# A long convolution by Fourier stages with a gated convolution behind it: late outputs, the order of products and taps, and the source of the taps

## The chip, the cores and the metric

The kernel runs on one core of one Trainium2 chip. The core has TensorE (PE, with PEld for its weight loads), VectorE (DVE), ScalarE (ACT), GpSimd (POOL) and SyncE (SP), which here issues every DMA. The metric is device microseconds per execution; the median of several runs counts.

## The reference

Eight sequences x[b] of 6400 x 128 are convolved with one long filter h of 6400 x 128, channel by channel (an FFT of double length, cut to 6400). What comes out, a, goes through a gated layer:

```
y    = irfft(rfft(x, 2S) * rfft(h, 2S))[:S]              # per channel
pre  = sum over k<5 of conv_w[k] * y[t-4+k]              # a short causal convolution, per channel
out  = (sigmoid(pre) * (y @ w_val)) @ w_out
```

All is float32.

## The kernel before

The long convolution is done as a real transform of length 6400 = 100 x 64, in four matrix stages on PE. The spectrum of h is computed once. For each of the eight sequences (batches) there are two stages in the program, and PE, DVE, ACT and POOL all keep the written order of their own instructions.

**First stage**, 16 groups (`for g in range(NS)`, line 584). Each group does the third transform of this batch (`s3_quads`: 64 matmuls from `gy` into two single PSUM banks, copied to `dt` by ACT and by DVE) and the first transform of the next batch (`fx.half`, 16 times 2 matmuls from `sd` into a pair of banks, copied to `gy` by ACT). POOL makes the sums and differences `sd` of the loaded x for it (`fx.sums`).

**Second stage**, 13 steps (`for s in range(NCH)`, line 611). Each step has

- a *product* for the next batch: the second transform on PE (`Product`, into a PSUM pair, of which there are two), two multiplications with the filter's spectrum on DVE (`mul_u` writes `gy`, `mul_t` writes `h`), and two additions on POOL (`add`, `gy` from `gy` and `h`);
- a *chunk* of this batch's result: the fourth transform on PE (`s4`, from `m4_sb` and `dt` into a single bank). The chunks are the head (positions 60 to 63 of 64) and 1 to 12, of five positions each.

What follows a chunk is the gated layer. ACT makes `copies` (y, to SBUF, in `dt` or `yl`, and two of the five taps of the short convolution, times their weights, one of them into the small buffer `p`). DVE adds three more *taps* (`more`: SCALAR_TENSOR_TENSOR, out = in x weight + out), POOL adds the fifth from `p`. PE projects y by w_val (`project`), ACT applies the sigmoid (`sigm`), DVE multiplies (`gate`), PE multiplies by w_out (`output`), ACT copies the result and SP stores it (`store`). A chunk's taps run one step after its fourth transform, its projection and gate two after, its output three after, its store four after.

Chunks 8 to 12 (positions 35 and up) are *late* in all batches but the last: in the second stage they are only copied to `yl`, and taps, projection, gate, output and store of these five and of the head come in the next batch's first stage (`Gates.trail`).

PSUM has four single banks, handed out in turn to the third transform, fourth transform, projection and output; a bank is free when its last reader is done. The taps of chunks that are not late, and of the head, read their chunk's PSUM bank.

Before the first batch there is a prologue: the first transform of h and of batch 0, and then, step by step, the spectrum of h and the products of batch 0. Between these products DVE decodes the gated layer's weights from their eight-byte form (`weights`, two operations a step). The tables of the fourth transform (`m4_sb`, thirteen pieces of 375 KB) are loaded in the first stage of batch 0, one a group.

Of the kernel before, what the change touches and what calls it, by code (L numbers as in the profile page):

```python
# [16 lines left out]
C = 128  # L17
# [3 lines left out]
HR = N1 // 2  # L21
HP = 64
MW = 3 * HR
SB = 4
NKB = 13
TAPS = 5
# [3 lines left out]
CH = 5  # L30
HEAD = (60, 4)
CHUNKS = [HEAD] + [(a, CH) for a in range(0, 60, CH)]
NCH = len(CHUNKS)
# [3 lines left out]
M2B = 3  # L37
# [73 lines left out]
def longconv_moe(ctx: ExitStack, tc: tile.TileContext, x, h, r1, m2, r3, m4, w64, out):  # L111
# [185 lines left out]
    class Spectrum:  # L297
# [72 lines left out]
    class Chunk:  # L370
# [33 lines left out]
        def copies(self):  # L404
            a, n = self.ch
            if a == HEAD[0]:
                for i, o in cells(0, n):
                    nc.gpsimd.memset(o[:, :, :1], 0.0)
                    self.first(4, o[:, :, 1:], self.p[:, i : i + n, : N1 - 1])
                act(self.y, self.p)  # L410
                for i, o in cells(a, n):
                    self.first(0, o, self.p)
                return
            if self.late:
                act(self.y, self.p)
                self.p = self.y
                return
            self.init()
            act(self.y, self.p)
            self.q = p_t[a // CH % 2]  # L420
            self.first(3, self.q, self.p)

        def init(self):
            a, n = self.ch
# [51 lines left out]
                        self.o[k * HP : (k + 1) * HP, i : i + o.shape[1]], lhsT=w, rhs=o, start=True, stop=True  # L476
                    )

        def store(self):
            act(self.y, self.o)  # L480
            i, k = _out_range(self.ch)
            nc.sync.dma_start(out[self.b, i:k].rearrange("(e n t) -> e n t", e=C, n=self.ch[1]), self.y)

# [25 lines left out]
    for kb in range(MH):  # L509
        m2_load(kb, m2_head)  # L510
    nc.sync.dma_start(r3_sb, r3)
    sp, pr = {0: Spectrum(0)}, {}
    for kb in range(-1, NKB + 1):
        if 0 <= kb < NKB:
            pr[kb] = Product(kb, sp[kb].h, t_head[kb % 3], m2_head)
            m2_load(kb + MH, m2_head)
        if kb + 2 < NKB:
            sp[kb + 2] = Spectrum(kb + 2)
        if kb + 1 < NKB:
            sp[kb + 1].copy()  # L520
            sp[kb + 1].store()
        if 0 <= kb < NKB:
            pr[kb].mul_u()
            pr[kb].mul_t()
            pr[kb].add(nc.vector if kb == NKB - 1 else nc.gpsimd)
            next(wgen, None)
            next(wgen, None)
    pairs.pop([p is ps2 for p in pairs].index(False))
    psp.__exit__(None, None, None)
    ps1 = ctx.enter_context(tc.tile_pool(name="ps1", bufs=4, space=bass.MemoryType.PSUM))  # L530

    class Gates:


        def __init__(self, b, defer):
            self.cs = [Chunk(b, ch, defer) for ch in CHUNKS]

        def trail(self):

            h, late = self.cs[0], [c for c in self.cs if c.late]  # L540
            steps = collections.defaultdict(list)
            for m, c in enumerate(late + [h]):
                t = 2 * m + 2
                if c is not h:
                    steps[t - 2].append(lambda c=c: c.taps(range(2)))
                    steps[t - 1].append(lambda c=c: c.taps(range(2, 4)))
                steps[t] += [c.project, c.sigm, c.gate]
                steps[t + 2].append(c.output)
                steps[t + 3].append(c.store)
            n = max(steps)  # L550
            return [lambda c=steps[i]: [f() for f in c] for i in range(n + 1)]

        def at(self, s, last):

            return self.cs[s] if 1 <= s < NCH else self.cs[0] if s == NCH and last else None

        def each(self, what, s, last=True):
            c = self.at(s, last)
            if c and not c.late:
                getattr(c, what)()  # L560

        def finish(self, s):
            self.each("project", s - 2)
            self.each("output", s - 3)
            self.each("store", s - 4)
            self.each("sigm", s - 2)
            if s == NCH:
                self.cs[NCH - 1].taps()
            self.each("gate", s - 2)

    trail = []
    fx = Forward(x[1], gy) if B > 1 else None
    if fx:
        fx.load(XB)
    for b in range(B):
        nxt = b + 1 < B


        if trail:
            trail.pop(0)()  # L580
        if nxt:
            for _ in range(2):
                fx.sums(nc.gpsimd)
        for g in range(NS):
            e = s3_quads(4 * g)
            f = []
            if nxt:
                f = fx.half()
                fx.sums(nc.gpsimd)
            e[0](act)  # L590
            e[1](dve)
            for u in f:
                u(act)
            if b == 0 and g < NKB:
                a = CH * g
                nc.sync.dma_start(m4_sb[:, a : a + CH], m4.rearrange("k (n t) -> k n t", t=MW)[:, a : a + CH])
            if nxt and g % 2 and g > 1:
                kb = g // 2 - 1
                if kb < M2B:
                    m2_load(kb)  # L600
                else:
                    h_load(kb - M2B)
            if trail:
                trail.pop(0)()
        if b + 2 < B:
            fx = Forward(x[b + 2], gy)


        gs = Gates(b, nxt)
        ps = {}  # L610
        for s in range(NCH):
            if s == 0:
                gs.cs[0].s4()
                gs.cs[0].copies()
                if nxt:
                    ps[0] = Product(0)
                    m2_load(M2B)
            if s == 1:
                gs.cs[s].s4()
            if nxt and s + 1 < NKB:  # L620
                ps[s + 1] = Product(s + 1)
                m2_load(s + 1 + M2B)
            gs.each("project", s - 2)
            if s > 1:
                gs.cs[s].s4()
            gs.each("output", s - 3)
            gs.each("store", s - 4)
            gs.each("sigm", s - 2)
            if s:
                gs.cs[s].copies()  # L630
            if nxt:
                ps[s].mul_u()
            if s > 1 and not gs.cs[s - 1].late:
                gs.cs[s - 1].taps()
            if nxt:
                ps[s].mul_t()
                ps.pop(s).add()
                h_load(s + HB)
            if s == 0:
                gs.cs[0].taps()  # L640
            gs.each("gate", s - 2)
            if s == 10 and b + 2 < B:
                fx.load(XB)
        trail = gs.trail() if nxt else [lambda s=s: gs.finish(s) for s in range(NCH, NCH + 5)]
    for t in trail:
        t()


def _lay_x(v):
# [42 lines left out]
```

## Time and profile before

| what | us |
|---|---|
| median of three runs | 1004.82 (1004.13 to 1008.4) |
| profiled execution, its own time | 1006.82 |
| its span | 1005.0 |
| first stage of the first batch (97.1 to 154.0) | 56.9 |
| usual first stage (328.5 to 380.9) | 52.4 |
| usual second stage (267.5 to 328.5) | 61.0 |
| last first stage, last second stage (900.8 to 946.4 to 1001.6) | 45.6, 55.2 |

A row of the page or of a view of groups gives engine, operation, what it writes and reads, sizes and count, then busy time, the mean ns of one, and the idle time of the engine before these instructions with what ended it. A row of a timeline gives start, duration, engine, operation, names, sizes and count, with an idle time before it in brackets. All instructions are issued through one helper, so that the line is the same for all (L98, and L99 in the changed kernel); names of tiles tell them apart.

### The profile page before, as it was taken

The numbers are of one execution on the slowest core, as the hardware profiler recorded it, in microseconds if no ns is written. First come the engines' busy times: TensorE is split into PE (matmuls) and PEld (weight loads), VectorE is DVE, ScalarE is ACT, GpSimd is POOL, SyncE is SP. The second block draws the span as 40 slices with busy tenths as digits, with TensorE's granted clock in tenths as the row PEclk, the third lists the DMA queues.
The fourth block names the chain that finished last, engine by engine and source line by source line (L and its number), as shares of the span: only waits on it lengthen the run. The fifth ranks groups of instructions, "written<-read, shape, count | busy, mean of one in ns | idle before, by whom it ended". The sixth has DMA issues, their size and how long they took to land.

```text
span 1005.0 us, 46982 instructions
## 1 busy us (share of the span) xinstructions
PE 940.5 (94%) x21360; PEld 793.5 (79%) x21360; DVE 702.8 (70%) x939; ACT 475.5 (47%) x916; POOL 544.5 (54%) x551
## 2 busy tenths in 40 slices
PE   7897778999999999999999998999989999999987
PEld 7797778787978878887878778887887878786753
DVE  5499217977398747977398756977399755978366
ACT  4521434445543653546444554445544553534465
POOL 6467434785277744785177743784367752760032
PEclk9898999999999999999999999999999999999989
DMA  7783854756467545755467555665467554750012
GB/s 253 244 272 149 283 204 158 225 157 194 134 229 214 156 154 194 230 159 166 150 223 218 153 159 186 216 176 170 145 211 221 151 178 159 229 140 34 31 42 91
DMA packets 96838, 177.33 MB, mean 176 GB/s; under 512 B 43392, under 2 KB 49792, under 8 KB 96640
## 3 DMA queue, kind: packets, MB, share of 16 engines
q1 hardware_dynamic: 96640, 174.34, 55.6%
q8 instruction: 167, 2.74, 1.1%
q14 instruction: 31, 0.25, 0.1%
HBM read 141.55 MB, written 32.77 MB: 173 GB/s over the span
## 4 chain that ended last, share of the span: by engine, by line
PE 90%; issue 5%; DVE 3%; POOL 1%; ACT 1%; DMA 0%; POOLq 0%; DVEq 0%; ACTq 0%
PE pt L98 90%; DVE gl L98 1%; DVE dt L98 1%; POOL gl L98 1%; ACT dt L98 1%; DVE gy L98 0%; POOL dt L98 0%; DMA x<-hl 0%; DVE sd L98 0%; DVE m_sb L98 0%; POOLq L688 0%; ACT gl L98 0%; ACT yl L98 0%; ACT gy L98 0%; DVEq L98 0%
## 5 line engine op out<-in xcount | busy, mean ns | idle before, releaser
L98 PE MATMUL pt<-r_sb,gy 64*64 64x128 f32 (+1 forms) x8192 | 267.3, 273 | 20.3 <-issue 11.5
L98 PEld LDWEIGHTS pt<-r_sb,gy 64*64 64x64 f32 (+1 forms) x8192 | 235.8, 130 | 63.8 <-ACT gl L98 20.4
L98 POOL TENSOR_TENSOR sd<-x 128x256 f32<-128x256 f32 x236 | 197.4, 860 | 154.2 <-issue 124.2
L98 POOL TENSOR_TENSOR gy<-gy,h 128x512 f32<-128x512 f32 (+1 forms) x182 | 221.6, 1241 | 63.6 <-DVE h L98 27.7
L98 ACT COPY dt<-pt 128x512 f32<-128x512 f32 (+3 forms) x269 | 155.2, 581 | 193.9 <-PE pt L98 191.6
L98 PEld LDWEIGHTS pt<-m_sb,dt 128*64 128x64 f32 x4096 | 191.5, 137 | 35.3 <-issue 22.7
L98 PEld LDWEIGHTS pt<-gy,m 128*64 128x64 f32 x3008 | 179.1, 135 | 43.8 <-issue 23.6
L98 PE MATMUL pt<-gy,m 128*64 128x128 f32 x3008 | 193.3, 278 | 17.5 <-issue 12.0
L98 PE MATMUL pt<-m_sb,dt 128*64 128x100 f32 x4096 | 198.0, 250 | 2.9 <-DVE dt L98 2.4
L98 DVE COPY dt<-pt 128x512 f32<-128x512 f32 (+1 forms) x136 | 92.5, 680 | 132.1 <-PE pt L98 125.6
L98 PE MATMUL pt<-r_sb,sd 50*64 50x100 f32 x4608 | 143.2, 258 | 17.2 <-issue 11.2
L98 DVE TENSOR_TENSOR gy<-pt,h 128x1024 f32<-128x1024 f32 (+1 forms) x99 | 116.8, 1180 | 46.3 <-PE pt L98 46.3
L98 DVE SCALAR_TENSOR_TENSOR gl<-yl,w_sb,gl 128x500 f32<-128x500 f32 x147 | 130.6, 892 | 24.6 <-ACT gl L98 22.1
L98 PEld LDWEIGHTS pt<-r_sb,sd 50*64 50x64 f32 x4608 | 128.9, 142 | 22.2 <-issue 14.5
L98 DVE SCALAR_TENSOR_TENSOR dt<-pt,w_sb,dt 128x500 f32<-128x500 f32 (+7 forms) x216 | 132.9, 631 | 13.5 <-POOL dt L98 3.8
L98 ACT COPY gy<-pt 128x400 f32<-128x400 f32 x248 | 110.2, 496 | 41.2 <-PE pt L98 32.8
L98 ACT ACTIVATE dt<-pt,w_sb 128x500 f32<-128x500 f32 (+1 forms) x64 | 40.0, 625 | 170.2 <-PE pt L98 169.4
L98 PE MATMUL pt<-dt,w_sb 128*64 128x500 f32 (+2 forms) x480 | 116.0, 561 | 0.8 <-DVE dt L98 0.4
L98 POOL TENSOR_TENSOR dt<-dt,p 128x500 f32<-128x500 f32 (+1 forms) x64 | 66.4, 1038 | 82.5 <-DVE dt L98 58.0
L98 DVE TENSOR_TENSOR h<-pt,h 128x1024 f32<-128x1024 f32 (+1 forms) x91 | 107.3, 1179 | 2.3
L98 ACT COPY yl<-pt 128x500 f32<-128x500 f32 (+1 forms) x96 | 54.5, 568 | 83.9 <-PE pt L98 83.9
L98 DVE TENSOR_TENSOR gl<-pt,gl 128x500 f32<-128x500 f32 (+1 forms) x48 | 31.7, 661 | 54.5 <-PE pt L98 50.8
(40 smaller groups left out, 568.5 us busy)
## 6 DMA issues: line engine op xcount, KB each, us to landing
m<-m SPq DMA_DIRECT2D x90, 512.0 KB, 4.7
h<-hd SPq DMA_DIRECT2D x84, 512.0 KB, 3.9
x<-xl SPq DMA_DIRECT2D x118, 256.0 KB, 3.4
out<-dt SPq DMA_DIRECT2D x56, 250.0 KB, 5.8
out<-yl SPq DMA_DIRECT2D x40, 250.0 KB, 2.5
m_sb<-m SPq DMA_DIRECT2D x13, 375.0 KB, 4.5
hd<-h SPq DMA_DIRECT2D x8, 512.0 KB, 5.1
m_sb<-m SPq DMA_DIRECT2D x6, 512.0 KB, 6.5
```

The lines of the kernel that those rows point to most:

```text
L98: return self._tc.keep_in_program_order(call(*args, **kwargs))
```

## The change

It has these parts.

1. Of the six outputs that stood in the next batch's first stage, those of late chunks 11 and 12 and of the head now stand in that batch's second stage, at its steps 0 and 1. The head's projection and gate come at group 13 of the first stage. The head's result is stored from one of the `p` buffers.
2. In a step of the second stage the two multiplications and POOL's additions now come ahead of the taps of the chunk before; the head's taps come at step 1, behind the second product, and not at step 0.
3. `copies` sets the chunk's source to the SBUF copy y, so that DVE's taps read it and not PSUM.
4. The weights' decode moves from the prologue's products to the first stage of batch 0. Four of the table loads move ahead, into the prologue's products, four stay in that first stage and five move to the second stage of batch 0.
5. In the last batch, DVE's copies of the third transform go to ACT, and projections start at step 5 of the second stage, by a list of steps.

```diff
@@ class Chunk: copies
-                return
-            if self.late:
+            else:
                 act(self.y, self.p)
-                self.p = self.y
-                return
-            self.init()
-            act(self.y, self.p)
-            self.q = p_t[a // CH % 2]
-            self.first(3, self.q, self.p)
+                if not self.late:
+                    self.init()
+                    self.q = p_t[a // CH % 2]
+                    self.first(3, self.q, self.p)
+            self.p = self.y
@@ prologue's products
+    def m4_load(j):
+        a = slice(CH * j, CH * j + CH)
+        nc.sync.dma_start(m4_sb[:, a], m4.rearrange("k (n t) -> k n t", t=MW)[:, a])
+
+    m4_rest = [12, 11, 10, 9, 4, 8, 5, 7, 6]
...
             pr[kb].add(nc.vector if kb == NKB - 1 else nc.gpsimd)
-            next(wgen, None)
-            next(wgen, None)
+        if 0 <= kb < M4H:
+            m4_load(kb)
@@ the first stage
+        for m, c in enumerate(pend[1:]):
+            steps[2 * m] += [lambda c=c: c.taps(range(2))]
+            steps[2 * m + 1] += [lambda c=c: c.taps(range(2, 4))]
+            steps[2 * m + 2] += [c.project, c.sigm, c.gate]
+            if m < 3:
+                steps[2 * m + 4] += [c.output]
+                steps[2 * m + 5] += [c.store]
+        if pend:
+            steps[13] += [pend[0].project, pend[0].sigm, pend[0].gate]
...
-            e[1](dve)
+            e[1](dve if nxt else act)
...
-            if b == 0 and g < NKB:
-                a = CH * g
-                nc.sync.dma_start(m4_sb[:, a : a + CH], m4.rearrange("k (n t) -> k n t", t=MW)[:, a : a + CH])
+            if b == 0:
+                next(wgen, None)
+                next(wgen, None)
+                if g % 3 == 0 and g < 12:
+                    m4_load(m4_rest.pop(0))
@@ the second stage
+        for i, c in enumerate(cs):
+            if i and not c.late:
+                jobs[i + 2 if nxt else (5, 6, 7, 8, 9, 10, 11, 11, 12, 13, 13, 14)[i - 1]].append(c)
+        if not nxt:
+            jobs[NCH + 1].append(cs[0])
...
+            if s == 0 and pend:
+                pend[0].output()
+                pend[0].store(p_t[1][:, : HEAD[1]])
...
+            late = pend[4 + s : 5 + s] if s < 2 else []
+            for c in outs + late:
+                c.output()
...
-            if nxt:
+            if s in ps:
                 ps[s].mul_u()
-            if s > 1 and not gs.cs[s - 1].late:
-                gs.cs[s - 1].taps()
-            if nxt:
                 ps[s].mul_t()
                 ps.pop(s).add()
                 h_load(s + HB)
-            if s == 0:
-                gs.cs[0].taps()
-            gs.each("gate", s - 2)
+            if 0 < s <= NCH and not cs[s - 1].late:
+                cs[s - 1].taps()
+            for c in jobs[s]:
+                c.gate()
```

How it moves instructions is seen at three places. On DVE, steps 4 and 5 of a second stage, before (`pt` is PSUM, `h` and `gy` belong to the product, `dt` holds y and the gate):

```order
TENSOR_TENSOR gy<-pt_2463,h_82 128x2x64x8
SCALAR_TENSOR_TENSOR dt<-pt_2484,w_sb,dt 128x5x100 x3
TENSOR_TENSOR h_82<-pt_2463,h_82 128x1024
TENSOR_TENSOR dt<-pt_2539,dt 128x5x100
TENSOR_TENSOR gy<-pt_2521,h_83 128x2x64x8
SCALAR_TENSOR_TENSOR dt<-pt_2542,w_sb,dt 128x5x100 x3
TENSOR_TENSOR h_83<-pt_2521,h_83 128x1024
```

and now:

```order
TENSOR_TENSOR gy<-pt_2461,h_82 128x2x64x8
TENSOR_TENSOR h_82<-pt_2461,h_82 128x1024
SCALAR_TENSOR_TENSOR dt<-dt,w_sb 128x5x100 x3
TENSOR_TENSOR dt<-pt_2539,dt 128x5x100
TENSOR_TENSOR gy<-pt_2520,h_83 128x2x64x8
TENSOR_TENSOR h_83<-pt_2520,h_83 128x1024
SCALAR_TENSOR_TENSOR dt<-dt,w_sb 128x5x100 x3
```

The three taps stood between the two multiplications and read `pt`; they now stand behind both and read `dt` alone.

On POOL, the same second stage from its start, before (`gy` is the product's addition, `dt<-dt,p` the fifth tap):

```order
TENSOR_TENSOR gy<-gy,h_82 128x64x8 x2
TENSOR_TENSOR gy<-gy,h_83 128x64x8 x2
TENSOR_TENSOR dt<-dt,p_92 128x100
TENSOR_TENSOR dt<-dt,p_92 128x4x100
TENSOR_TENSOR gy<-gy,h_84 128x64x8 x2
TENSOR_TENSOR dt<-dt,p_93 128x5x100
TENSOR_TENSOR gy<-gy,h_85 128x64x8 x2
```

and now:

```order
TENSOR_TENSOR gy<-gy,h_82 128x64x8 x2
TENSOR_TENSOR gy<-gy,h_83 128x64x8 x2
TENSOR_TENSOR gy<-gy,h_84 128x64x8 x2
TENSOR_TENSOR dt<-dt,p_92 128x100
TENSOR_TENSOR dt<-dt,p_92 128x4x100
TENSOR_TENSOR gy<-gy,h_85 128x64x8 x2
TENSOR_TENSOR dt<-dt,p_93 128x5x100
```

The two additions of a step now come ahead of the fifth tap of that step's chunk.

On PE, the first rows of a second stage in a later batch, before (`dt` rows are the fourth transform, `gy` rows the products):

```order
MATMUL pt_4013<-m_sb,dt 64x2x50 x16
MATMUL pt_4034<-gy,m_0_79 64x64x2 x16
MATMUL pt_4052<-gy,m_1_80 64x64x2 x16
MATMUL pt_4081<-m_sb,dt 64x2x50 x20
MATMUL pt_4102<-gy,m_2_81 64x64x2 x16
MATMUL pt_4128<-gy,m_0_79 64x64x2 x16
```

and now (`gl` rows are outputs):

```order
MATMUL pt_3998<-m_sb,dt 64x2x50 x16
MATMUL pt_4015<-gl,w_sb 64x400 x2
MATMUL pt_4020<-gy,m_0_79 64x64x2 x16
MATMUL pt_4038<-gy,m_1_80 64x64x2 x16
MATMUL pt_4056<-gl,w_sb 64x500 x2
MATMUL pt_4070<-m_sb,dt 64x2x50 x20
MATMUL pt_4091<-gy,m_2_81 64x64x2 x16
MATMUL pt_4109<-gl,w_sb 64x500 x2
```

One output, the head's, comes ahead of the first product; two more stand among the first steps.

More of the change, by code (lines that the diff above doesn't have):

```diff
@@ L23 @@
 MW = 3 * HR
+M4H = 4
 SB = 4
@@ L477, in output, with store @@
                     )
-        def store(self):
-            act(self.y, self.o)
+        def store(self, y=None):
+            y = self.y if y is None else y
+            act(y, self.o)
             i, k = _out_range(self.ch)
-            nc.sync.dma_start(out[self.b, i:k].rearrange("(e n t) -> e n t", e=C, n=self.ch[1]), self.y)
+            nc.sync.dma_start(out[self.b, i:k].rearrange("(e n t) -> e n t", e=C, n=self.ch[1]), y)
     wgen = weights()
@@ L530, in longconv_moe @@
     ps1 = ctx.enter_context(tc.tile_pool(name="ps1", bufs=4, space=bass.MemoryType.PSUM))
[L532 to L571, printed above, removed]
     fx = Forward(x[1], gy) if B > 1 else None
@@ L574, in longconv_moe @@
         fx.load(XB)
+    pend = []
     for b in range(B):
         nxt = b + 1 < B
-        if trail:
-            trail.pop(0)()
+        steps = collections.defaultdict(list)
+        for m, c in enumerate(pend[1:]):
[7 more added lines that the diff above has]
+            steps[13] += [pend[0].project, pend[0].sigm, pend[0].gate]
         if nxt:
@@ L602, in longconv_moe @@
                     h_load(kb - M2B)
-            if trail:
-                trail.pop(0)()
+            for u in steps[g]:
+                u()
         if b + 2 < B:
             fx = Forward(x[b + 2], gy)
-        gs = Gates(b, nxt)
-        ps = {}
-        for s in range(NCH):
-            if s == 0:
-                gs.cs[0].s4()
-                gs.cs[0].copies()
-                if nxt:
[L616 to L619, printed above, removed]
+        cs = [Chunk(b, ch, nxt) for ch in CHUNKS]
+        jobs = collections.defaultdict(list)
+        for i, c in enumerate(cs):
[3 more added lines that the diff above has]
+            jobs[NCH + 1].append(cs[0])
+        ps, outs = {}, []
+        for s in range(max(NCH - 1, *jobs) + 2):
+            if s < 2:
+                cs[s].s4()
+            if s == 0 and pend:
+                pend[0].output()
+                pend[0].store(p_t[1][:, : HEAD[1]])
+            if nxt and s == 0:
+                ps[0] = Product(0)
+                m2_load(M2B)
             if nxt and s + 1 < NKB:
@@ L622, in longconv_moe @@
                 m2_load(s + 1 + M2B)
[L623 to L630, printed above, removed]
-            if nxt:
+            if m4_rest:
+                m4_load(m4_rest.pop(0))
+            for c in jobs[s]:
+                c.project()
+            if 1 < s < NCH:
+                cs[s].s4()
+            late = pend[4 + s : 5 + s] if s < 2 else []
+            for c in outs + late:
+                c.output()
+            for c in jobs[s]:
+                c.sigm()
+            if s < NCH:
+                cs[s].copies()
+            for c in outs + late:
+                c.store()
+            if s in ps:
                 ps[s].mul_u()
-            if s > 1 and not gs.cs[s - 1].late:
-                gs.cs[s - 1].taps()
-            if nxt:
                 ps[s].mul_t()
@@ L638, in longconv_moe @@
                 h_load(s + HB)
-            if s == 0:
-                gs.cs[0].taps()
-            gs.each("gate", s - 2)
+            if 0 < s <= NCH and not cs[s - 1].late:
+                cs[s - 1].taps()
+            for c in jobs[s]:
+                c.gate()
+            outs = jobs[s]
             if s == 10 and b + 2 < B:
                 fx.load(XB)
-        trail = gs.trail() if nxt else [lambda s=s: gs.finish(s) for s in range(NCH, NCH + 5)]
-    for t in trail:
-        t()
+        pend = [cs[0]] + [c for c in cs if c.late]
 def _lay_x(v):
```

## The prediction

> **What bounds the kernel now.** I read the page's busy line and chain first, then the windows of single stages, then the engines' timelines inside one second stage.
>
> ```profile
> PE 940.5 (94%) x21360; PEld 793.5 (79%) x21360; DVE 702.8 (70%) x939; ACT 475.5 (47%) x916; POOL 544.5 (54%) x551
> PE 90%; issue 5%; DVE 3%; POOL 1%; ACT 1%; DMA 0%; POOLq 0%; DVEq 0%; ACTq 0%
> ...
> 97.10:154.00 56.90, 44.63 (x1520) 41.95 (x1523) 11.64 (x16) 22.25 (x46) 23.68 (x33) 0.94 0.63 216
> 328.50:380.90 52.40, 52.13 (x1571) 42.75 (x1572) 31.95 (x42) 31.59 (x64) 27.13 (x32) 1.00 0.49 154
> 900.80:946.40 45.60, 42.76 (x1075) 31.72 (x1072) 28.16 (x42) 18.18 (x34) 0.00 (x0) 1.00 0.10 36
> ...
> 267.50:328.50 61.00, 58.50 (x1002) 50.35 (x994) 51.68 (x67) 24.68 (x47) 40.85 (x37) 1.00 0.69 211
> 946.40:1001.60 55.20, 49.15 (x622) 31.28 (x620) 38.10 (x63) 35.81 (x67) 15.45 (x15) 0.94 0.18 53
> ```
>
> In the windows the columns are busy time of PE, PEld, DVE, ACT and POOL, then clock, DMA share and GB/s. TensorE is 90% of the chain. A usual first stage (328.5) has 0.3 us of PE idle in 52.4, a usual second stage (267.5) 2.5 in 61.0. The three odd stages are the first first stage (97.1: 12.3 idle) and the two of the last batch. But the second stage is tight on a second engine: DVE is busy 51.7 us of 61. Its middle shows how tight (DVE, then PE, then POOL):
>
> ```profile
> 293.86 1.22 DVE L98 TENSOR_TENSOR gy<-pt,h 128x1024 f32<-128x1024 f32 x1
> 294.99 2.28 DVE L98 SCALAR_TENSOR_TENSOR dt<-pt,w_sb,dt 128x500 f32<-128x500 f32 x3
> 297.19 1.22 DVE L98 TENSOR_TENSOR h<-pt,h 128x1024 f32<-128x1024 f32 x1
> 298.32 0.67 DVE L98 TENSOR_TENSOR dt<-pt,dt 128x500 f32<-128x500 f32 x1
> 298.90 1.22 DVE L98 TENSOR_TENSOR gy<-pt,h 128x1024 f32<-128x1024 f32 x1
> ...
> 298.70 2.01 PE L98 MATMUL pt<-gy,m 128*64 128x128 f32 x32
> 300.54 1.01 PE L98 MATMUL pt<-dt,w_sb 128*64 128x500 f32 x4
> 301.38 1.89 PE L98 MATMUL pt<-m_sb,dt 128*64 128x100 f32 x40
> 303.10 1.01 PE L98 MATMUL pt<-dt,w_sb 128*64 128x500 f32 x4
> ...
> 298.65 2.53 POOL L98 TENSOR_TENSOR gy<-gy,h 128x512 f32<-128x512 f32 x2
> ```
>
> From start to start, one step of DVE is 1.13 (first product) + 2.20 (three taps) + 1.13 (second product) + 0.58 (gate) = 5.04 us without a gap. One step of PE is 1.84 (product) + 0.84 (projection) + 1.72 (fourth transform) + 0.84 (output) = 5.24. So PE leads by 0.2 us a step, and 0.2 us is all that DVE may lose. The product's PSUM pairs are two, so the product of step s+2 waits for the second multiplication of step s: if DVE's step is the longer, PE goes at DVE's pace.
>
> **The taps, which decide.** The change makes every tap of the second stage read the SBUF copy, so both its tensors are in SBUF, and it puts the taps right behind the second multiplication, which is what releases POOL's two additions. Before, the taps read PSUM, and the rows above show POOL's 2.53 us beside undisturbed products and taps. What a DVE instruction with both tensors in SBUF meets beside POOL is seen elsewhere in this trace:
>
> ```profile
> 228.84 1.51 DVE L98 SCALAR_TENSOR_TENSOR gl<-yl,w_sb,gl 128x500 f32<-128x500 f32 x2
> ...
> 218.88 2.42 DVE L98 SCALAR_TENSOR_TENSOR gl<-yl,w_sb,gl 128x500 f32<-128x500 f32 x2
> ...
> 215.28 7.30 POOL L98 TENSOR_TENSOR sd<-x 128x256 f32<-128x256 f32 x8
> ...
> 91.18 0.42 DVE L98 TENSOR_TENSOR gl<-gl 128x261 int32<-128x261 int32 x1
> 91.63 1.37 DVE L98 TENSOR_TENSOR w_sb<-gl 128x261 f32<-128x261 f32 x1
> ...
> 96.50 1.87 DVE L98 TENSOR_TENSOR gy<-gy,m_sb 128x256 f32<-128x256 f32 x2
> ...
> 91.40 2.73 POOL L98 TENSOR_TENSOR gy<-gy,m_sb 128x512 f32<-128x512 f32 x2 [1.27 <-DVE m_sb L98]
> ...
> L98 POOL TENSOR_TENSOR gy<-gy,h 128x512 f32<-128x512 f32 x11 | 13.9, 1286 | 0.0
> ```
>
> Two SBUF taps take 1.51 us with POOL quiet, as long as from PSUM, and 2.42 beside a run of POOL's 256-wide sums: 0.45 lost per tap. Beside the very addition in question, an operation of one size goes from 0.42 to 1.37: 0.95 lost behind one POOL instruction. Two such operations in a row, at 96.50, take 1.87 and not 0.84. In the changed order the first tap starts before POOL has its signal (as at 91.18, 91.40 and 91.63), the first addition goes in between and the second tap waits, then the second addition and the third tap. That is two losses a step. Behind the taps on DVE stand the gate and the next step's products, and PE waits for these. I take 0.95 each, the row with the same POOL instruction; the bounds are 0 (DVE keeps going and POOL waits) and the instruction's whole 1.286.
>
> [...]
>
> So DVE's step becomes 5.04 + 1.9 = 6.94 us against PE's 5.24. A whole second stage, on the clock of the one at 267.5, needs its first steps:
>
> ```profile
> 271.86 1.23 DVE L98 TENSOR_TENSOR gy<-pt,h 128x1024 f32<-128x1024 f32 x1 [3.58 <-PE pt L98]
> ...
> 274.33 0.52 DVE L98 SCALAR_TENSOR_TENSOR gl<-pt,w_sb,gl 128x300 f32<-128x300 f32 x1
> ...
> 276.32 1.21 DVE L98 TENSOR_TENSOR gy<-pt,h 128x1024 f32<-128x1024 f32 x1
> ...
> 278.71 1.22 DVE L98 TENSOR_TENSOR gy<-pt,h 128x1024 f32<-128x1024 f32 x1
> 279.84 2.40 DVE L98 SCALAR_TENSOR_TENSOR dt<-pt,w_sb,dt 128x400 f32<-128x400 f32 x6
> 282.15 1.22 DVE L98 TENSOR_TENSOR h<-pt,h 128x1024 f32<-128x1024 f32 x1
> ...
> 275.12 2.05 PE L98 MATMUL pt<-gy,m 128*64 128x128 f32 x31
> 278.89 2.08 PE L98 MATMUL pt<-gy,m 128*64 128x128 f32 x32 [1.73 <-issue]
> ...
> 283.47 2.07 PE L98 MATMUL pt<-gy,m 128*64 128x128 f32 x32 [0.78 <-PE pt L98]
> ```
>
> DVE starts 0.84 later, at 272.70, because the head's output stands ahead of the first product. Products of steps 0 and 1 end at 272.70 + 2.47 + 2.39 = 277.6 (the starts at 271.86, 274.33, 276.32, 278.71). Head taps 1.99 + 1.9: 281.5. Step 2: 2.28 + (2.31 + 1.9) = 287.9. Steps 3 to 8: 6 x 6.94, and 0.2 for chunks cut in two: 329.8. Step 9's products, 2.28: 332.1, and this lets PE start product 11; it then has 1.84 (that product), 1.72, 0.84, 0.92 (the half product 12), and two transforms of 1.72 left: 340.9. Before, the next first stage began at 328.5. So a second stage grows by 12.4 us. The two PE stalls shown (1.73 and 0.78), which the reordering would remove, and the PE time of the three moved outputs are inside this chain and count no more. Seven stages: **+87**.
>
> **What the rest gains.** Three outputs leave each first stage:
>
> ```profile
> L98 PE MATMUL pt<-gl,w_sb 128*64 128x500 f32 x20 | 5.3, 608 | 0.0
> ```
>
> Five outputs are 5.3 us of PE, overlaps counted in, so three give 3.2 at most and 0.84 each at least; I take 2.9, in six PE-bound first stages: **-17.5** (bounds -15 and -19). Their copies go to ACT, busy 24.7 us of the second stage's 61. Their stores, 750 KB, go into SP's queue there beside the loads of the next products, which have a buffer to spare, all the more in a longer stage.
>
> First stage of the first batch, and the start:
>
> ```profile
> L98 PE MATMUL pt<-r_sb,gy 64*64 64x128 f32 x512 | 31.7, 287 | 11.8 <-issue 6.5 <-DVE gy L98 5.2
> ...
> m_sb<-m SPq DMA_DIRECT2D x13, 375.0 KB, 4.5
> ...
> 97.11 0.70 PE L98 MATMUL pt<-r_sb,gy 64*64 64x128 f32 x8 [5.24 <-DVE gy L98]
> ```
>
> Most of PE's idle here, beside the first wait, is "issue", in the one first stage whose DMA share is 0.63 and not 0.49. 216 GB/s over 56.9 us are 12.3 MB; nine of the thirteen table loads leave it, 3.4 MB, and 8.9 remain, near the 8.1 of the usual stage, which idles 0.3 us. I estimate that 4 of the 12.3 remain: **-8** (bounds 0, if the loads are not the cause, and -11). The decode's two operations a group cost at most 2 x 1.37 us on a DVE that is busy 22 of 57, so they are hidden there. In the product phase they made DVE late: PE waits 5.24 us at 97.11. Without the last 1.37 and 0.42 and the lag before them the wait shrinks by some 2, and four table loads come in: **-1.5** (bounds -3 and +2). The other five loads stand in the first batch's second stage, where each is issued three steps or more ahead of the transform that reads it: nothing.
>
> Last batch: its first stage loses three outputs and part of the waits for ACT (its PE idles 2.8 us), while ACT, busy 18 us of 45, takes 16 more copies from DVE: **-3.5** (bounds -6 and +2). The second stage there is a chain of taps, POOL addition and taps:
>
> ```profile
> 983.61 2.29 DVE L98 SCALAR_TENSOR_TENSOR gl<-pt,w_sb,gl 128x500 f32<-128x500 f32 x3 [0.85 <-POOL gl L98]
> ...
> 987.33 2.29 DVE L98 SCALAR_TENSOR_TENSOR gl<-pt,w_sb,gl 128x500 f32<-128x500 f32 x3 [0.85 <-POOL gl L98]
> ```
>
> 3.72 us a chunk, which the new order keeps: each chunk's taps still follow the POOL addition of the one before. There are no products there, so nothing of POOL's runs beside them. **-1** (bounds -4 and +2).
>
> Sum: 87 - 17.5 - 8 - 1.5 - 3.5 - 1 = +55.5. The profiled execution took 1006.82 us (span 1005.0), the median of the runs 1004.82: 1062 and **1060 us**, 5.5% slower.
>
> **The rivals.** First, the taps lose nothing: DVE holds its turn through three taps and POOL, which has 20 us to spare in a second stage, waits. Then DVE's step stays 5.04, the stage is PE's own 58.5 + 3 x 0.84 = 61.0 as before, and the other terms stand: 1004.8 - 31.5 = 973 us. For it: it is POOL that has time to spare, and no row shows three SBUF taps in a row beside the long additions. Against it: the two operations in a row at 96.50, with an addition of the same size beside them, lost 1.0. 0.12.
>
> Second, each loss is only the 0.45 seen beside the narrower sums. 0.9 a step instead of 1.9, over eight steps: a second stage grows by 4.4, seven by 31, and that cancels the gains: 1004 us. It speaks for it that this price is of the same tap instruction; against it, that this POOL instruction holds 1.286 and not 0.73 us. 0.06. It also names the turning point: 0.91 lost per step, and the change costs nothing.
>
> Third, the whole 1.286 twice, 2.57 a step: a stage grows by 17.8, the sum is +93: 1098 us. 0.04.
>
> **How the numbers follow.** The forecast has 0.78. Its own range, 1040 to 1085, comes from losses of 0.8 to 1.1 and the bounds of the smaller terms. To leave out no more than the first rival and part of the other two, the range is 1015 to 1088. About 0.5% (5 us) is what a measurement of this kernel can tell from none. Faster: 0.12, the first rival. Within: 0.06, the second. Slower: the rest, 0.82.
>
> **What would show it.** In the new profile, taps of the second stage (dt from dt) near 1.37 us on the mean and not 0.74, three of them 4 us long, the additions of POOL between them; DVE without gaps over steps 1 to 9; PE waiting once a step for a PSUM pair; second stages of about 73 us, first stages of about 49.5, the first of them near 49. I am wrong at the decisive step if the second stages last 61 us, and wrong in the price if they lie between 62 and 70.

## The result, and the profile after

The changed kernel takes 1096.28 us (median of 4 runs, 1094.67 to 1101.79), beside 1006.4 for the kernel before (4 runs, 1004.13 to 1008.4): a ratio of 1.090 (95% interval 1.085 to 1.095). The forecast was 1060 with a range of 1015 to 1088. The direction was right, and the loss is 90 us where 55 had been forecast.

The profiled execution took 1101.79 us with a span of 1100.0, 95 more than the 1005.0 before. Busy line and chain of the page:

```profile
PE 957.0 (87%) x21360; PEld 802.3 (73%) x21360; DVE 787.5 (72%) x923; ACT 487.3 (44%) x932; POOL 582.4 (53%) x551
PE 51%; DVE 28%; issue 14%; DMA 3%; ACT 2%; POOL 1%; SPq 0%; DVEq 0%; POOLq 0%
```

TensorE had 90% of the chain, and now has 51%. DVE went from 3% to 28%. That DVE would set the pace was the forecast. "Issue" went from 5% to 14%, and that was not. The groups by form, the second stage's taps and POOL's additions:

```profile
L99 DVE SCALAR_TENSOR_TENSOR dt<-dt,w_sb 128x500 f32<-128x500 f32 x128 | 152.1, 1188 | 15.3 <-POOL dt L99 6.9
...
L99 POOL TENSOR_TENSOR gy<-gy,h 128x512 f32<-128x512 f32 x168 | 247.6, 1498 | 147.2 <-PE pt L99 86.9 <-issue 55.8 <-DVE h L99 4.6
```

In the same view of the kernel before these means are 738 and 1283 ns. Both engines are held up.

The windows of single stages (columns as before: PE, PEld, DVE, ACT, POOL, clock, DMA share, GB/s): the first first stage, a usual first and second stage, and the last two:

```profile
99.50:156.70 57.20, 46.47 (x1522) 44.39 (x1526) 20.56 (x38) 22.27 (x46) 24.29 (x33) 0.88 0.47 154
...
359.60:412.10 52.50, 50.04 (x1552) 41.60 (x1554) 31.69 (x42) 29.83 (x60) 28.10 (x33) 1.00 0.50 164
412.10:486.80 74.70, 62.11 (x1016) 51.58 (x1008) 66.43 (x67) 26.95 (x50) 45.69 (x36) 1.00 0.56 165
...
998.70:1039.20 40.50, 39.10 (x1062) 30.58 (x1060) 18.96 (x27) 24.05 (x45) 0.33 (x1) 1.00 0.07 23
1039.20:1096.10 56.90, 49.78 (x636) 32.35 (x632) 37.97 (x62) 37.29 (x71) 15.60 (x15) 0.97 0.20 60
```

Read in the same way for all stages (a first stage goes from its first matmul of the third transform to its last, and a second stage from there to the next), the span divides like this:

| part of the span | before | after | difference | forecast |
|---|---|---|---|---|
| up to the first first stage | 97.1 | 99.5 | +2.4 | -1.5 |
| first stage of the first batch | 56.9 | 57.2 | +0.3 | -8 |
| six first stages | 319.8 | 320.0 | +0.1 | -17.5 |
| seven second stages | 427.0 | 522.1 | +95.0 | +87 |
| last batch's first stage | 45.6 | 40.6 | -5.0 | -3.5 |
| last batch's second stage | 55.2 | 56.9 | +1.7 | -1 |

The loss was sized almost right. What is missing are the gains: 31 us of them did not come.

**Inside a second stage.** DVE, POOL and PE in one step of the changed kernel:

```profile
312.90 1.21 DVE L99 TENSOR_TENSOR gy<-pt,h 128x1024 f32<-128x1024 f32 x1
314.14 1.23 DVE L99 TENSOR_TENSOR h<-pt,h 128x1024 f32<-128x1024 f32 x1
315.28 4.06 DVE L99 SCALAR_TENSOR_TENSOR dt<-dt,w_sb 128x500 f32<-128x500 f32 x3
319.27 0.67 DVE L99 TENSOR_TENSOR dt<-pt,dt 128x500 f32<-128x500 f32 x1
319.86 1.21 DVE L99 TENSOR_TENSOR gy<-pt,h 128x1024 f32<-128x1024 f32 x1
...
315.50 3.31 POOL L99 TENSOR_TENSOR gy<-gy,h 128x512 f32<-128x512 f32 x2 [1.76 <-issue]
...
319.99 1.94 PE L99 MATMUL pt<-m_sb,dt 128*64 128x100 f32 x40 [1.66 <-DVE dt L99]
```

A step is 312.90 to 319.86 = 6.96 us without a gap on DVE, and 6.94 were forecast. The three taps take 315.28 to 319.27 = 3.99 us where they took 2.20, and POOL's two additions lie between them and take 3.31 where they took 2.53. PE waits for DVE. In the stage's first steps that is at the product, as predicted (1.23 us at 315.42). From the next step on it is at the fourth transform, 1.5 to 1.7 us, for the PSUM bank that DVE's gate frees (here at 319.94).

**Inside a first stage.** SP, PE and POOL of the changed kernel (a row with "x3" is three issues in a row):

```profile
351.53 4.94 SPq L99 DMA_DIRECT2D out<-dt  x2
356.52 14.47 SPq L99 DMA_DIRECT2D x<-xl  x9
...
394.37 0.34 SPq L99 DMA_DIRECT2D out<-yl  x1
394.96 0.33 SPq L99 DMA_DIRECT2D x<-xl  x1
395.34 1.40 SPq L99 DMA_DIRECT2D h<-hd  x3
...
401.74 1.36 PE L99 MATMUL pt<-r_sb,gy 64*64 64x128 f32 x41 [1.32 <-issue]
...
362.03 0.92 PE L99 MATMUL pt<-r_sb,sd 50*64 50x100 f32 x32 [0.31 <-POOL sd L99]
...
360.57 7.80 POOL L99 TENSOR_TENSOR sd<-x 128x256 f32<-128x256 f32 x10 [0.65 <-DMA x<-xl]
```

And SP in the kernel before:

```profile
317.11 3.90 SPq L98 DMA_DIRECT2D out<-dt  x2
321.07 1.68 SPq L98 DMA_DIRECT2D x<-xl  x3
...
360.83 0.41 SPq L98 DMA_DIRECT2D h<-hd  x1
...
367.55 0.34 SPq L98 DMA_DIRECT2D out<-yl  x1
367.94 0.43 SPq L98 DMA_DIRECT2D h<-hd  x1
374.30 0.34 SPq L98 DMA_DIRECT2D out<-yl  x1
374.69 0.94 SPq L98 DMA_DIRECT2D h<-hd  x1
```

PE's busy time in the stage did fall, from 52.13 to 50.04 us, by 2.1 of the forecast 2.9 (three outputs left). Its idle time rose from 0.3 to 2.5. Over the six stages the busy time fell by 10.6 (313.2 to 302.6) and the idle time rose by 10.8 (6.6 to 17.4). Two things changed on SP, to which the program gives every DMA, in this order, and each store behind its result (in the kernel before SP's waits for the copies to `yl` add up to 213.3 us, in 47 waits). Before, a store of a late output stood between any two `h` loads (512 KB each), and its wait spread them 6 to 7 us apart (360.83, 367.94, 374.69). Now three of them leave within 1.4 us (at 395.34). And the first `x` loads of the next batch, at 321.07 before, well ahead of the stage that starts at 328.50, now stand behind a store whose output is made in the same step, at 356.52 for a stage that starts at 359.6: POOL's sums wait for the data (0.65 us at 360.57) and PE for the sums (0.31 at 362.03). In the second stage the changed kernel stores a chunk in the step of its output; before, it did so one step after it.

### The profile page after: what moved, and what is told of

Its sections match the earlier page's. It is cut to its first block, busy times and chain, and to the rows that moved or that the text cites. A ratio compares the mean times of both kernels' runs of the same rounds, so it can differ in the third digit from the quotient of the medians.

```text
span 1100.0 us, 47118 instructions
## 1 busy us (share of the span) xinstructions
PE 957.0 (87%) x21360; PEld 802.3 (73%) x21360; DVE 787.5 (72%) x923; ACT 487.3 (44%) x932; POOL 582.4 (53%) x551
## 3 DMA queue, kind: packets, MB, share of 16 engines
q8 instruction: 168, 2.75, 1.0%
## 4 chain that ended last, share of the span: by engine, by line
PE 51%; DVE 28%; issue 14%; DMA 3%; ACT 2%; POOL 1%; SPq 0%; DVEq 0%; POOLq 0%
PE pt L99 51%; DVE dt L99 16%; DVE gy L99 7%; DVE gl L99 3%; DMA x<-xl 2%; DVE h L99 1%; ACT dt L99 1%; POOL sd L99 1%; DVE sd L99 0%; DMA x<-hl 0%; SPq L99 0%; ACT p L99 0%; ACT gl L99 0%; POOL dt L99 0%; ACT yl L99 0%
## 5 line engine op out<-in xcount | busy, mean ns | idle before, releaser
L99 POOL TENSOR_TENSOR gy<-gy,h 128x512 f32<-128x512 f32 (+1 forms) x182 | 257.2, 1440 | 147.2 <-PE pt L99 86.9
L99 PE MATMUL pt<-r_sb,gy 64*50 64x128 f32 (+1 forms) x8192 | 269.4, 275 | 23.6 <-issue 17.7
L99 PEld LDWEIGHTS pt<-r_sb,gy 64*50 64x50 f32 (+1 forms) x8192 | 237.6, 131 | 63.7 <-issue 27.4
L99 ACT COPY dt<-pt 128x512 f32<-128x512 f32 (+3 forms) x285 | 162.9, 581 | 231.0 <-PE pt L99 230.8
L99 DVE SCALAR_TENSOR_TENSOR dt<-dt,w_sb 128x500 f32<-128x500 f32 (+2 forms) x192 | 201.3, 1065 | 15.7 <-POOL dt L99 6.9
L99 DVE SCALAR_TENSOR_TENSOR gl<-yl,w_sb,gl 128x500 f32<-128x500 f32 (+2 forms) x187 | 158.8, 853 | 32.4 <-ACT gl L99 26.8
L99 DVE COPY dt<-pt 128x512 f32<-128x512 f32 (+1 forms) x120 | 81.4, 679 | 126.0 <-PE pt L99 119.5
L99 PE MATMUL pt<-r_sb,sd 50*64 50x100 f32 x4608 | 147.1, 263 | 20.8 <-issue 10.5
L99 ACT ACTIVATE dt<-dt 128x500 f32<-128x500 f32 (+1 forms) x64 | 36.4, 571 | 196.5 <-POOL dt L99 196.5
L99 ACT COPY yl<-pt 128x500 f32<-128x500 f32 (+1 forms) x89 | 51.0, 573 | 86.6 <-PE pt L99 80.5
```

The source lines that it names most:

```text
L99: return self._tc.keep_in_program_order(call(*args, **kwargs))
```

## The experiments

Unless said otherwise an edit is made to the changed kernel. Medians of the kernel before on the same chips were 1004.44 (the first four runs), 1004.66 (the next four) and 1006.08 (the last four).

### Where the taps read, and the order

**The changed kernel with its taps back on PSUM:**

```diff
-            self.p = self.y
+            if self.late:
+                self.p = self.y
```

> The changed kernel with one part undone: the taps of chunks that are not late read PSUM again. If the loss is DVE's two-SBUF-input taps taking turns with POOL's additions, the three taps take 2.3 us again and not 3.9 to 4.1, DVE's step goes from 6.96 to 5.04 to 5.3, the second stages from 74.7 to 61 to 63 us, and the time from 1096 to 1000 to 1012. If it is the new order (taps behind both multiplications) that makes DVE the bound whatever the taps read, the second stages stay above 70 and the time above 1060. In both cases the first stages stay at 52 to 54.

Measured: 995.23, ratio 0.990 (0.987 to 0.993). The windows of a second and a first stage:

```profile
268.20:328.40 60.20, 60.20 (x1021) 55.65 (x1013) 51.88 (x67) 27.18 (x50) 40.49 (x36) 1.00 0.69 206
328.40:381.50 53.10, 49.75 (x1553) 41.71 (x1556) 31.02 (x42) 29.84 (x61) 26.90 (x32) 1.00 0.50 161
```

The source of the taps costs 101 us (1096.28 to 995.23), more than the whole loss. With them gone the second stage has no PE idle at all. The first stages stay as they were, 52.2 to 55.6 us: their trouble has nothing to do with the taps.

**The kernel before with only its taps moved to the SBUF copy, in the old order:**

```diff
                     self.first(0, o, self.p)
+                self.p = self.y
                 return
...
             self.first(3, self.q, self.p)
+            self.p = self.y
```

> The kernel before with one part of the change: the taps read the SBUF copy, in the old order between the two multiplications. If what is lost is the overlap in time with POOL's additions, less is lost here, since the two additions (2.5 us) begin beside the gate and the first multiplication (1.7 us) and only their end meets the first tap: one loss of 0.5 to 0.9 a step, a DVE step of 5.6 to 5.9 against PE's 5.24, second stages of 63 to 66 us, 1020 to 1045 in all. If any SBUF tap beside any POOL work loses the same, it is as slow as the changed kernel, 1085 to 1100.

Measured: 1068.42, ratio 1.064 (1.061 to 1.068). A second stage, and DVE and POOL in a step:

```profile
280.90:350.40 69.50, 59.51 (x1002) 49.95 (x992) 60.27 (x67) 24.65 (x47) 41.70 (x37) 1.00 0.59 185
...
313.38 3.35 DVE L98 SCALAR_TENSOR_TENSOR dt<-dt,w_sb 128x500 f32<-128x500 f32 x3
316.65 1.22 DVE L98 TENSOR_TENSOR h<-pt,h 128x1024 f32<-128x1024 f32 x1
...
311.99 2.53 POOL L98 TENSOR_TENSOR gy<-gy,h 128x512 f32<-128x512 f32 x2
```

Here the additions start ahead of the taps. The first tap, at 313.38, meets the second of them, which ends at 314.52: 3.27 us for three taps where 2.20 was usual, a loss of 1.07, by my estimate all in the one tap that meets an addition. In the changed order it is 1.79 in two losses. So the source is the cause and the order sets how many losses there are. My expectation had one loss a step, but of 0.9 at most, and its top was 23 us too low: a stage grew by 8.5 to 9.3 us and not by the 5 of that end.

**The kernel before with only the new order, taps on PSUM:**

```diff
-            if s > 1 and not gs.cs[s - 1].late:
-                gs.cs[s - 1].taps()
             if nxt:
                 ps[s].mul_t()
                 ps.pop(s).add()
                 h_load(s + HB)
-            if s == 0:
-                gs.cs[0].taps()
+            if s and not gs.cs[s - 1].late:
+                gs.cs[s - 1].taps()
```

> The kernel before with the other part: multiplications and additions ahead of the taps, head taps at step 1, taps from PSUM. If PSUM taps lose nothing beside POOL, DVE's step stays at 5.04, the stalls of 1.73 and 0.78 us at the start of a second stage shrink, second stages last 59.5 to 61 us and the time is 993 to 1006. If the order alone makes DVE late, the second stages are above 63 and the time above 1020.

Measured: 992.55, ratio 0.988 (0.986 to 0.990). A second and a first stage, and a step of DVE and POOL:

```profile
267.30:326.20 58.90, 58.27 (x1003) 50.61 (x994) 51.78 (x67) 25.53 (x47) 40.31 (x36) 1.00 0.73 219
326.20:380.60 54.40, 52.47 (x1571) 42.69 (x1571) 32.23 (x42) 31.48 (x64) 28.07 (x33) 1.00 0.49 148
...
301.18 2.28 DVE L98 SCALAR_TENSOR_TENSOR dt<-pt,w_sb,dt 128x500 f32<-128x500 f32 x3
...
301.39 2.52 POOL L98 TENSOR_TENSOR gy<-gy,h 128x512 f32<-128x512 f32 x2 [1.43 <-PE pt L98]
```

The order by itself is worth 12 us: PE's 2.5 us of idle in a second stage, the two stalls at its start, shrink to 0.6. It fits that the run above and the one below came out some 5 us under their expected ranges, which had left this gain out. And the same taps in the same place beside the same additions, but with one of their tensors in PSUM, lose nothing: 2.28 us for three, and 2.29 at 983.61 in the kernel before, where nothing of POOL's runs beside them.

**The changed kernel without POOL's two additions in the second stage.** This leaves out part of the complex product (the sums of its partial products), so its time tells only of the taps:

```diff
-                ps.pop(s).add()
+                ps.pop(s)
```

> The changed kernel without POOL's two additions in each step of the second stage (products of batches 1 to 7 are left without them; the prologue keeps them). If the additions are what the taps wait for, each SBUF tap takes 0.74 us again, DVE's step is 5.0 to 5.1 and the second stages last 60 to 62 us: 1000 to 1010 in all. If the SBUF copies are slow to read for another reason (ACT, PE or DMA on the same memory), the taps stay above 1.2 us and the stages above 70.

Measured: 994.26 (one run). The group of the taps, and a second stage:

```profile
L99 DVE SCALAR_TENSOR_TENSOR dt<-dt,w_sb 128x500 f32<-128x500 f32 x128 | 94.1, 736 | 16.0 <-POOL dt L99 7.0 <-PE pt L99 0.5 <-DVE dt L99 0.5
...
264.70:324.80 60.10, 60.10 (x1016) 53.69 (x1008) 51.88 (x67) 27.04 (x50) 9.32 (x10) 1.00 0.70 207
```

SBUF taps take 736 ns when these additions are away, as from PSUM (738 before), and 1188 with them. POOL's addition of the fifth tap, 1.25 us a step, is still there and does no harm. In the changed kernel it runs beside DVE's gate and the next first multiplication, which read PSUM (POOL from 319.52, DVE from 319.27 and 319.86), and these take 0.67 and 1.21 us there; the second multiplication, at 314.14 with nothing of POOL's beside it, takes 1.23.

### The first stages

**The four `h` loads of a first stage issued by ACT, one every two groups,** so that SP's order no longer bunches them:

```diff
-    def h_load(kb):
+    def h_load(kb, e=nc.sync):
...
-            nc.sync.dma_start(h_sb[kb % HB][:, :n], hd[kb, :, :n])
+            e.dma_start(h_sb[kb % HB][:, :n], hd[kb, :, :n])
...
-                    h_load(kb - M2B)
+                    h_load(kb - M2B, nc.scalar)
```

> The changed kernel, with the four loads of the filter's spectrum in each first stage issued by ACT at their groups 9, 11, 13 and 15, not by SP, where three of them go out within 1.5 us now that fewer stores stand between them. If this burst holds up the fetch of PE's instructions, the gap of 1.3 to 2.5 us that PE shows 41 to 44 us into each first stage goes, the first stages last 50 to 51.5 us and not 52.4 to 54.4, the first of them 53 to 55, and the time falls from 1096 by 14 to 22. If the gap has another cause, the stages stay at 52 to 54 and the time within 5 us of the changed kernel's.

Measured: 1081.61, ratio 1.073 (1.069 to 1.078; one of the four executions took 2387.79, which nothing in the kernel explains: it counts in this median but not in the ratio, and the median of the other three is 1080.25). The first first stage, a usual one, and a second stage:

```profile
98.70:150.80 52.10, 45.39 (x1521) 43.27 (x1524) 20.53 (x38) 22.25 (x46) 24.30 (x33) 0.90 0.49 159
350.30:399.90 49.60, 49.21 (x1554) 41.45 (x1556) 31.33 (x42) 30.02 (x61) 27.67 (x33) 1.00 0.52 161
399.90:474.50 74.60, 62.04 (x1016) 51.52 (x1007) 66.39 (x67) 26.95 (x50) 45.63 (x36) 1.00 0.57 172
```

14.7 us less by the medians. The six first stages fall from 320.0 to 304.5, so the -17.5 of the forecast is nearly there (-15.4 against the kernel before), and the first batch's first stage falls from 57.2 to 52.1. PE's idle time in the six is 6.7 us, as in the kernel before (6.6); the 15.4 is busy time of PE alone (313.2 to 297.8). The second stage does not move. This edit changes two things at once, the spacing of the loads and the queue that issues them; no run spreads them on SP.

**The kernel before with its four `h` loads issued together,** at group 9 of each first stage:

```diff
-                else:
-                    h_load(kb - M2B)
+                elif kb == M2B:
+                    for i in range(HB):
+                        h_load(i)
```

> The kernel before, with the four loads of the filter's spectrum of each first stage issued together at group 9 and not at 9, 11, 13 and 15. If a burst of loads holds up PE's instructions, a gap of 1.5 to 2.5 us appears in each first stage some 5 us behind it, and the time grows by 8 to 16: 1012 to 1020. If not, 1002 to 1008.

Measured: 1015.71, ratio 1.009 (1.006 to 1.012). The longest of its six first stages, SP and PE:

```profile
447.20:502.70 55.50, 52.52 (x1567) 42.70 (x1568) 32.32 (x42) 31.50 (x64) 27.22 (x32) 1.00 0.45 155
...
480.42 2.13 SPq L98 DMA_DIRECT2D h<-hd  x4
...
486.64 0.57 PE L98 MATMUL pt<-r_sb,sd 50*64 50x100 f32 x16 [1.28 <-issue]
```

The burst alone brings the "issue" gap behind it into the old kernel too: 6 us after it, as in the changed kernel (395.34 to 401.74). Five of the six stages show such a gap, of 0.5 to 2.0 us; it ends 6 to 10 us after the first load of the burst. One stage shows none. The loss is 11 us, but only 5 of them lie in the six first stages (324.8 against 319.8). 4 lie ahead of the first stage of the first batch, where nothing was edited, so this run supports the cause and does not size it. What PE waits for is not in its records, but the traces hold transfers of instructions, 16 KB pieces on a queue of their own (`q8 instruction: 168, 2.75, 1.0%` on the changed kernel's page: 168 pieces, 2.75 MB). In the first stages of all fourteen traces PE has 146 gaps of over 0.5 us without a releaser. Every one of them ends 2.2 to 3.5 us after the latest of these pieces started, 137 of them 2.1 to 2.7 us after it; a moment taken at random in these stages lies so far behind a piece 13% of the time. In the rows above a piece starts at 484.30 and PE goes on at 486.64; in the changed kernel it is 399.12 and 401.74. My estimate from these lags is that PE was out of instructions in these gaps; no record shows which engine a piece was for.

Whether the loads are what holds a piece up is less sure. Among the pieces that start 2 to 14 us after the first `h` load of a stage, the longest spacing is 5.4 to 7.5 us in the changed kernel and 5.5 to 8.1 with the burst here, but 3.8 to 5.9 with the loads on ACT and 5.1 to 6.5 in the kernel before. A spacing of 6.5 alone made no gap there (351.80 to 358.31, in the stage that starts at 328.5). That the pieces stood behind 1.5 MB of loads fits this; it is my estimate, and no run tested it by itself.

**Both repairs, taps on PSUM and `h` loads on ACT:**

> As e1_psum_taps (taps from PSUM), with the same four loads issued by ACT. If the two losses are separate, first stages of 50 to 51.5 us beside second stages of 60.2: 973 to 983. If the burst is not the cause, 990 to 1000 as e1_psum_taps.

Measured: 977.84, ratio 0.973 (0.969 to 0.977). The six first stages take 50.2 to 51.4 us each and the second stages 60.1 to 60.6 (the first batch's 58.8). The two repairs add up.

**The same with the next batch's `x` loads ahead of the store, one step earlier:**

```diff
+            if s == 9 and b + 2 < B:
+                fx.load(XB)
             for c in outs + late:
                 c.store()
...
-            if s == 10 and b + 2 < B:
-                fx.load(XB)
```

> As e6_psum_act, with the first three x loads of the next batch issued one step earlier, ahead of the store behind which they wait on SP. If PE's gap of 0.3 to 1.6 us at 2 us into the first stages (sums that wait for x) comes from there, it goes and a first stage is 0.5 to 1.2 us shorter: 3 to 7 us less than e6_psum_act. If x is not late for that reason, no change.

Measured: 970.85, ratio 0.966 (0.962 to 0.970), the best of the study; run again beside the next three it took 972.92, 0.968 (0.963 to 0.972). PE's wait for POOL's first sums is gone from its records. The gain by the medians is 7 us; the two profiled executions were alike (977.17 and 977.33), so its size is not settled.

### Decode, table loads and the last batch

Each of these undoes one part in that best version, beside a run of it on the same chip:

> The base of the three runs beside it, unchanged: taps from PSUM, h loads on ACT, x loads one step earlier. 969 to 978, as before; it gives the base on the same chip.

Measured: 972.92 (971.21 to 976.23). Its first first stage, a second stage, and the last one:

```profile
97.10:148.00 50.90, 43.57 (x1519) 41.26 (x1523) 20.59 (x38) 22.23 (x46) 24.31 (x33) 0.94 0.50 163
256.60:316.70 60.10, 60.10 (x1016) 55.58 (x1008) 51.90 (x67) 27.15 (x50) 40.77 (x37) 1.00 0.75 223
909.70:967.20 57.50, 50.22 (x632) 33.19 (x632) 37.22 (x62) 37.30 (x71) 15.45 (x15) 0.94 0.20 59
```

**The decode back between the prologue's products:**

```diff
             pr[kb].add(nc.vector if kb == NKB - 1 else nc.gpsimd)
+            next(wgen, None)
+            next(wgen, None)
...
-                next(wgen, None)
-                next(wgen, None)
```

> The version of the last run (taps from PSUM, h loads issued by ACT, x loads one step earlier) with the weights' decode back between the prologue's products. By the prediction (DVE is late at the end of the prologue because of the decode) PE's wait at the first instruction of the first stage grows from 3.4 to about 5.2 us, the first stage begins 2 later and the kernel is 2 us longer, some 973 if the base is 971. Rival: the decode is hidden in the prologue too, and the time is within 1 us of the base.

Measured: 973.62, 0.968 (0.964 to 0.972). The wait at the start of the first stage is 5.26 us and not 3.41, as foreseen:

```profile
100.23 0.70 PE L99 MATMUL pt<-r_sb,gy 64*64 64x128 f32 x8 [5.26 <-DVE gy L99]
```

The median moved by 0.7 only, which this measurement can't tell from nothing: the place of the cost is shown, a gain in the total is not.

**All thirteen table loads back in the first stage of the first batch:**

```diff
-    m4_rest = [12, 11, 10, 9, 4, 8, 5, 7, 6]
+    m4_rest = list(range(NKB))
...
-        if 0 <= kb < M4H:
-            m4_load(kb)
...
-                if g % 3 == 0 and g < 12:
+                if m4_rest:
                     m4_load(m4_rest.pop(0))
```

> The same version with all thirteen table loads back in the first stage of batch 0, one a group. By the prediction (the loads cause the issue gaps there) that stage grows from 49.9 by 5 to 8 us and the prologue loses at most 2: 975 to 978 if the base is 971. Rival: the gaps come from the h loads, which are on ACT here, and from the products' table loads; then the first stage stays within 2 us and the prologue, with a lower DMA share, is up to 2 us shorter: 969 to 972.

Measured: 978.55, 0.973 (0.968 to 0.977): 5.6 us more than beside it.

```profile
97.70:152.40 54.70, 44.06 (x1517) 41.37 (x1521) 20.57 (x38) 22.25 (x46) 24.32 (x33) 0.94 0.66 215
```

The stage grows by 3.8, from 50.9 to 54.7, with the DMA share going from 0.50 to 0.66: the loads were a cause of its gaps, and moving them is worth about half of the forecast 8 (with the tables moved it takes 49.3 to 51.7 in the five profiles with taps on PSUM and loads on ACT). The start of the stage moves by 0.6 us, which is within the spread of the starts, so the four loads in the prologue cost nothing that shows.

**The last batch's old schedule** (projections two steps behind, every second copy of the third transform on DVE):

```diff
-            e[1](dve if nxt else act)
+            e[1](dve)
...
-                jobs[i + 2 if nxt else (5, 6, 7, 8, 9, 10, 11, 11, 12, 13, 13, 14)[i - 1]].append(c)
+                jobs[i + 2].append(c)
```

> The same version with the last batch's old schedule: projections two steps behind the fourth transform, and every second copy of the third transform on DVE. By the prediction the reordering of the last batch is worth 1 to 3 us (the three outputs that left the last first stage stay away): 972 to 974 if the base is 971. Rival: it is worth nothing or a loss, 968 to 971.

Measured: 972.08, 0.965 (0.960 to 0.970), no difference.

```profile
872.20:912.70 40.50, 39.04 (x1061) 30.55 (x1060) 28.15 (x42) 16.71 (x30) 0.00 (x0) 1.00 0.07 23
912.70:968.20 55.50, 49.99 (x632) 32.18 (x632) 38.02 (x63) 37.13 (x70) 15.42 (x15) 0.97 0.22 65
```

The last first stage is as short with DVE's copies as with ACT's (40.5 and 40.4), so its 5 us come from the outputs that left it. The window of the last second stage is 2 us shorter in the old schedule, but behind it the span goes on for 4.5 us (968.2 to 972.7) and not 3.5 (967.2 to 970.7), and the medians differ by 0.8. So the reordering there brings no gain that shows, and a loss of 1 us or less is not settled.

## Why the prediction was right and wrong

**Right: the taps.** The step that was to decide held: DVE's step of 6.94 us measured 6.96, the taps have POOL's additions between them, DVE has no gaps over steps 1 to 9, PE waits on it (in most steps for the bank that the gate frees and not for the product's pair, which changes no term of the sum). The row that set the price was read rightly too: the decode's operation that took 1.37 us beside POOL takes 0.43 in the changed kernel's first stage. That POOL's additions are the other party is shown by leaving them out (736 ns, stage 60.1), and that two SBUF tensors are the condition by putting the taps back (60.2). The first rival (the taps hold their turn and lose nothing) is refuted. The second (0.45 a loss) was too cheap. The third (1.286 twice, 1098 us) came out nearest in time and for the wrong reason: its step would have been 7.6 us.

**A little small: the second stage as a whole,** +12.4 forecast and +13.7 measured for a usual one. The chain on DVE came out 0.9 longer over its start and its eight steps (the products of step 9 end 65.5 us into the stage, not 64.6), and the rest is PE's start behind the last of them. Over seven stages 8 us of the 39 that the sum missed.

**Wrong: "three outputs leave each first stage: -17.5".** The term came out at +0.1. The step that failed took PE's work out of the stage and looked no further along SP's queue than the stores' bytes, which were sent to the second stages. The work did leave (2.1 us of PE in the stage shown). But the stores had been what held SP back between the `h` loads, and without their waits the loads went out together. The runs put the price at 15 us over the six stages (the loads on ACT), and the same bunching made the old kernel slower, by 5 us in its six first stages. How the 15 divide between the bunching and the other queue is open. A second hand in it was the `x` loads behind a store, whose part lies between nothing and 7 us.

**Half right, and hidden: "-8" in the first stage of the first batch.** The table loads do cause part of its gaps, but 3.8 us and not 8. In the changed kernel even that was eaten up by the bunched `h` loads (57.2 us, and 52.1 with the loads on ACT), by their largest gap of all:

```profile
145.36 2.08 PE L99 MATMUL pt<-r_sb,gy 64*50 64x128 f32 x33 [3.73 <-issue]
...
140.00:148.00 8.00, 4.27 (x123) 4.01 (x118) 1.00 (x2) 2.06 (x4) 1.41 (x2) 0.76 0.36 134
```

This stage has no late outputs, before or after, so it is not stores that left here. In the kernel before, its last three `h` loads went out at 137.66 to 139.65 with a table load between them, and the gap that followed was 1.18 us (to 144.59). Now they go out at 136.19 to 137.94, and it is 3.73. Why it grew so much is open.

**Hidden by the start: "-1.5" up to the first stage.** It came out at +2.4, though the wait at its end did shrink, from 5.24 to 3.38 us. The first products started at 47.75 and not 45.47, ahead of anything that the change touches; over the profiled executions of this study it lies between 45.1 and 49.0 with the same program up to there (the two ends are the old kernel with the new order and with the burst). So this term's sign can't be read from the start of the stage. Counted from the first product, the way to the first stage is 51.6 to 53.2 us in the five traces with the decode in the prologue and 50.5 to 51.8 in the nine without it, 52.3 and 51.1 on the mean. That is 1.2 us the way that was forecast, though the two sets overlap.

**The last batch,** -4.5 forecast and -3.3 measured: the outputs gave 5.0 where 3.5 was forecast, and the last stage came out 1.7 longer where it was to be 1 shorter; the run with its old schedule won back about 1 us of that.

The range failed mainly because its upper end took every gain as near certain. With the gains at nothing, a bound that I had not put on the largest of them, the sum would have been 1005 + 87 = 1092 us.

## What to carry to other kernels

In this kernel the stores, which only move data out, were what paced the loads behind them on SP's queue: `h` loads 6 to 7 us apart with them, three within 1.4 us without. Before moving such an instruction, write down what the queue will issue back to back once it is gone, and how far ahead of its reader each load then lands. And before a VectorE operand moves from PSUM to SBUF, look what GpSimd does in that stretch: here, with one operand in PSUM, the two ran side by side for nothing (three taps in 2.28 us with the additions beside them, in 2.29 without), and with both in SBUF each meeting cost about 0.9 to 1.1 us.

## What the runs showed of the hardware that was not expected

- Behind three loads of 512 KB that leave together, PE's stream has a gap with no visible releaser in every first stage of the changed kernel, of 0.8 to 2.5 us and once 3.7, which ends 5 to 9 us after the first of them. With the same loads spread out on ACT the six stages run with 0.4 to 2.0 us of idle instead of 2.3 to 3.5.
- All 146 gaps without a releaser of over 0.5 us in the first stages end 2.2 to 3.5 us after a 16 KB piece of instructions starts on its way. That PE is out of instructions there is my estimate from this.
- Around the longest of these gaps PE's granted clock stood at 0.76 over 8 us (the row above), and the matmuls from 145 to 151 us took 0.37 to 0.42 us on the mean where they take 0.25 to 0.28 just before and after, so this gap cost more than its own length.
- Where taps with both tensors in SBUF met POOL's additions, both engines lost: the additions went from 1283 to 1498 ns on the mean, while the taps went from 738 to 1188.
